# Crossbar transposes for a linear-attention hand-over, and new constants for a planned four-layer kernel

## The chip, the cores and the metric

The kernel runs on one core of a Trainium2 chip. The metric is the device time of one execution in microseconds (us). The core has five engines that run their own instruction lists: TensorE (PE, matrix products), VectorE (DVE), ScalarE (ACT), GpSimd (POOL) and SyncE (SP, which here only issues transfers). Sixteen DMA engines move data beside them. Matrix products land in PSUM, eight banks of 128 x 512 floats; everything else lies in SBUF.

## The reference, cut to what matters

Four layers run over one sequence of 2048 rows of 512 numbers: softmax attention (A), linear attention (B), A again, B again, each with a layer norm before it and a residual addition behind it. A has 32 query heads of 16 numbers and one shared key and value head.

```python
def _A_ref(x, wq, wk, wv, wo):            # H = 32, Dh = 16
    ...
    scores = jnp.einsum("bhqd,bkd->bhqk", q, k) * (Dh ** -0.5)
    p = _softmax(scores, axis=-1)
    o = jnp.einsum("bhqk,bkd->bhqd", p, v)
    ...
def _B_ref(x, wqkv, wo):
    ...
    kv = jnp.einsum("bhsd,bhse->bhde", pk, v)
    num = jnp.einsum("bhqd,bhde->bhqe", pq, kv)
    den = jnp.einsum("bhqd,bhd->bhq", pq, z)[..., None] + 1e-6
    ...
x = A_x
x = x + _A_ref(_layernorm(x, axis=-1), A_wq, A_wk, A_wv, A_wo)
x = x + _B_ref(_layernorm(x, axis=-1), B_wqkv, B_wo)
x = x + _A_ref(_layernorm(x, axis=-1), A_wq, A_wk, A_wv, A_wo)
x = x + _B_ref(_layernorm(x, axis=-1), B_wqkv, B_wo)
```

The dominant work is the exponential of 32 x 2048 x 2048 scores in each of the two softmax layers.

## The kernel before, in words

**Tiles.** The sequence is 16 tiles of 128 rows. In a softmax layer the scores are made in blocks of 128 keys x 512 columns, where a column is a query row of one of four heads. A layer has 32 segments (16 query tiles, times two halves of the heads) with 16 x 4 blocks each, which is 2048 blocks for a layer and 4096 for the kernel.

**Two ways for a block.** A score block (L990, four 32-row products beside each other on PE) leaves PSUM either through ACT or through DVE. ACT exponentiates two or three blocks with one instruction (L1170) into a tile named PT; one product (L1044) then multiplies it with the values. DVE takes a single block (L1256): it adds a constant and clamps, and the bits of the 16-bit integer, read as bf16, are a straight-line approximation of the exponential. Three more copies of it with an offset, each for four blocks at once (L1304), and a weighted sum of four products make the approximation good. One of these three copies can be made by DMA instead of DVE: POOL fills a buffer with the offset from a constant row in DRAM (L1328, "priming") and later issues a transfer that adds the block to it (L1337, an "addition"). Tile names in the trace are those of the memory that a buffer borrows: FB, xn, wq, wo, sacc, OBB and xnT all serve as such buffers for a while.

**The planner.** The order of each engine's instructions isn't written by hand. When the kernel is built, a class Planner (L36 to L353) plays the program through with a cost for each operation, a priority, and pools of banks and buffers; whenever a planned engine comes free, it takes the eligible operation with the lowest priority number. What comes out is one fixed list for each engine, with semaphore waits. So constants that look like costs change no instruction's speed; they change the order, which engine takes a copy, and how many blocks and copies go which way. Those that the change touches:

- SWITCH: what a change between PE's row, column and full tile shapes costs in the plan. STICK: how far the plan goes out of order to stay in one shape.
- TRS, TRT, DXF, DTAIL: how long a transposing DMA and an addition take in the plan. While a transposing DMA is in flight there, POOL starts no transfer (L158), and later POOL transfers wait for the last six of them (L200).
- BLS, BLT, BLO, DXB: how much work may be queued for DVE when it is given another block. A block gets there in three ways: as third member of a group whose banks belong to ACT, which leaves ACT two (dve_split, L1246, bounds BLS and BLT); as an additional member in a free bank (dve_open, L1240, BLO); or in a product of its own in a free bank (alone, L1266, DXB).
- FBO, FBS, FBP, AHEAD, NPRE, DQ, DMIN: how many buffers must be free for a new group of four, for a copy, for priming; how far ahead copies run; when an addition may be chosen (L1291: something is primed, the segment isn't among the last DMIN, and the planned DMA queue ends within DQ).
- CHE, CHT, ENDL, BACK: where DVE stops taking blocks ahead of a layer's end, and when borrowed weight buffers are called back. LAG: how close a more urgent operation must be for an engine to wait for it.

Constants set for layer 0 stay in force until layer 2 sets its own.

**The hand-over that the change is about.** It runs from layer 1 (linear) to layer 2 (softmax). Layer 1's sums over the keys need all 16 tiles of layer 0, so its second part, main(t), starts only when layer 0 is over. For a tile, main(t) multiplies the query side with the sums (L1838), divides into a tile OBB (L1842), transposes it in four 128 x 128 pieces on PE with an identity matrix (L1857), copies the result from PSUM to SBUF (L1860, recorded as L746; ACT or DVE, as the planner chooses), multiplies with the output weights (L761) and adds to x (L1870). Layer 2 follows for the same tile: statistics (L842, L843), two small POOL steps (L844, L846), the normalized tile xn (L849), four transposes on PE (L869), a copy into xnT (L874, recorded as L746), then the products for values, keys and queries (L757, L761, L923). Tiles 0 and 1 take a split path of their own (L789, L1824). From the third tile on, main(t) waits in the plan until layer 2's xnT of tile t-2 is there (MGATE, MLAG, L1796). In layer 2 ACT begins exponentials as soon as the first two key tiles are there, in the order of SEQ (L416): key tiles 0 and 1 for query tiles 0 and 1, then key tiles 2 and 3, then query tiles 2 and 3 on key tiles 0 to 3, then key tiles 4 to 7 for four query tiles, then 8 to 15. Keys are made for tiles 0, 1, 2-3, 4-7, 8-11 and 12-15 (KG, L417). DVE takes blocks only once the keys of tile 15 are there (KGATE).

**Transposes by DMA** are there already: dmat (L767) issues one from SP, and ln_tile(far) uses it for layer 0's tiles 4 to 15 (FARA, first entry). The same branches exist for layer 2 (FARA, second entry, L884) and for main(t) (FARM, L1848).

Of the kernel before, what the change touches and what calls it, by code (L numbers as in the profile page):

```python
# [35 lines left out]
class Planner:  # L36
# [43 lines left out]
    def op(self, opts, reads=(), writes=(), prio=5.0, lat=0.08, dma=False, name="", join=None, mode="full", port=False, after=(), behind=(), xfer=None, trn=False):  # L80

        o = Op()
        o.opts, o.prio, o.users, o.done, o.end = opts, prio, [], False, None
        o.eng, o.fn, o.n, o.value, o.sem, o.signal, o.isdma = None, None, None, None, None, False, dma
        o.name = (name, lat)
        o.freed = False
        o.begun = None
        o.cols = 0
        o.mode = mode
        o.port = port  # L90
        o.xfer = xfer
        o.trn = trn
        deps = set()
        for k in reads:
            deps.update(self.ws(k))
        for k in list(writes) + list(after) + list(behind):
            deps.update(self.ws(k))
            deps.update(self.readers.get(k, ()))
        if join is not None:
            deps.update(join.deps)  # L100
            deps.discard(join)
        for k in writes:
            if join is not None and join in self.ws(k):
                self.writer[k] = self.ws(k) + [o]
            else:
                self.writer[k] = [o]
                self.readers[k] = []
        for k in list(reads) + list(after):
            if k not in writes:
                self.readers.setdefault(k, []).append(o)  # L110
        o.deps = deps
        o.left = 0
        chain = len(opts) == 1 and PE in opts
        for d in deps:
            if not (d.done or (chain and d.freed and d.eng == PE)):
                o.left += 1
                d.users.append(o)
        if o.left == 0:
            self._eligible(o)
        return o  # L120
# [26 lines left out]
    def _dispatch1(self, e):  # L147
# [4 lines left out]
        while h:  # L152
# [24 lines left out]
            if e == PE:  # L177
                if self.mode != o.mode:
                    dur += max(SWITCH - (self.now - self.until[e]), ROWIN if o.mode == "row" else 0.0)
                self.mode = o.mode  # L180
# [13 lines left out]
            if o.trn:  # L194
                self.turning.append(o)
                self.turned = self.turned[-5:] + [o]
                self.dmaq = max(end, self.dmaq) + TRS
                end = self.dmaq + TRT
            if o.xfer:
# [156 lines left out]
class Seg:  # L356
# [11 lines left out]
    def take(self, js, back=False):  # L368
# [12 lines left out]
QK_DUR = 0.22  # L381
PV_DUR = 0.222
QK_LAT = 0.438
SWITCH = 0.107
ROWIN = 0.025
PV_LAT = 0.215
EX_LAT = 0.185
# [3 lines left out]
LAG = 0.15  # L391
# [7 lines left out]
DMAX = 1.0  # L399
RING = 24  # L400
NOB = 4
TRS = 1.4
TRT = 1.0
FARA = (4, 16)
FARB = 0
FARO = 0
FARM = {1: (), 3: ()}
GROW = (5,)
BLS = 1.4
BLO = 5.0  # L410
DXB = 2.0
BLT = 2.5
# [12 lines left out]
ENDL = 12  # L425
# [7 lines left out]
FBO = 2  # L433
FBS = 4
AHEAD = 20
CHT = 19
PSH = False
STICK = 0.8
PBL = 1.2
BACK = 2  # L440
PRING = 8
DSH = 1
DMIN = 4
NPRE = 2
EVEN = True
CHE = 8
AVOID = True
PGEN = 0.95
DPF = 1.7
DXF = 3.2  # L450
DTAIL = 2.0
DQ = 4.0
FBP = 4
TUNE = {0: {"CHE": 2, "AHEAD": 10, "BLS": 1.7, "FBP": 2, "NPRE": 1, "DMIN": 3, "LAG": 0.1, "STICK": 2.0, "FBO": 1, "FBS": 4, "BLO": 7.0, "DXB": 0.8, "BLT": 3.2},
        2: {"CHE": 6, "CHT": 16, "FBS": 2, "AHEAD": 15, "BLO": 3.5, "DXB": 2.5, "FBP": 3, "DMIN": 2, "STICK": 0.8, "LAG": 0.1, "DQ": 5.0}}


def bass_interleave_layers__grouped_kv_mqa__linear_attn_block__prompt_kernel(
# [111 lines left out]
    def guest(L, kind, i, h=None):  # L570
        return once((L, kind, i, h), home[kind, i]) if (kind, i) in home else ()
# [103 lines left out]
    def reload(dst, src, writes, prio, behind):  # L675
        return op({PO: (1.1, lambda e: e.dma_start(dst, src))}, writes=writes, prio=prio, lat=0.3, dma=True, behind=behind, xfer=(2.4, DTAIL))

# [34 lines left out]
    def fb_keys(i):  # L712
        return [("FB", i, h) for h in range(CHB)]
# [53 lines left out]
    def dmat(dst, src, reads, writes, prio, after=()):  # L767
        return op({SP: (0.1, lambda e: e.dma_start(dst, src, transpose=True))}, reads=reads, writes=writes, prio=prio, lat=0.5, dma=True, behind=after, trn=True)

    def until(*keys):  # L770
        for k in keys:
            yield ("ops", pl.ws(k))
# [105 lines left out]
    def a_tile(L, t, prio):  # L878
# [4 lines left out]
        cr = t in MCRIT[L - 1] if L else False  # L883
        yield from ln_tile(L, t, prio, t >= FARA[L // 2], cr)  # L884
        pl.flag(("xnT", L, t))
# [95 lines left out]
    def run_a(L):  # L981
# [23 lines left out]
        def spend(h, o):  # L1005
            h[0] -= 1
            if o not in h[1]:
                h[1].append(o)
            if h[0] == 0:
                pl.give_after(h[2], h[3], h[1])  # L1010
# [85 lines left out]
        def act_stream():  # L1096
            if L == 0:
                globals().update(TUNE[0])
            yield ("flag", ("K", L, 0))
            globals().update(TUNE[L])  # L1100
            if L:
# [214 lines left out]
        def prime():  # L1316
# [6 lines left out]
            while state["si"] < len(segs) - DMIN:  # L1323
                if len(primed) >= NPRE or len(fb_pool.free) <= FBP or fb_pool.wait:
# [3 lines left out]
                o = op({PO: (PGEN, lambda e, g_=g_: e.dma_start(fbs[g_].bitcast(I16), cst.to_broadcast([P, CHB * 512])))}, reads=["cst"], writes=fb_keys(g_), prio=9.0,  # L1328
                       lat=0.3, dma=True, behind=guest(L, "FB", g_), xfer=(DPF, DTAIL))
                primed.append((g_, o))  # L1330
# [4 lines left out]
        def dma_shift(blk, f_, hold, g_, o):  # L1335
            pl.stat["dma"] += 1
            o = op({PO: (PGEN, lambda e: e.dma_start(fbs[g_].bitcast(I16), fbs[f_].bitcast(I16), accum_op=ALU.add))}, reads=fb_keys(f_), writes=fb_keys(g_), prio=0.0, lat=0.3,  # L1337
                   dma=True, xfer=(DXF, DTAIL))
            spend(hold, o)
# [152 lines left out]
    def run_b(L):  # L1492
# [299 lines left out]
        def main(t):  # L1792
# [52 lines left out]
            pl.give_after(banks, b, [o])  # L1845
            if t not in FARM[L]:
                yield from until(("OB", i, 0), ("OB", i, 1))
            if t in FARM[L]:  # L1848
                dmat(OTB[:, i, :, :], OB[:, i, :], [("OB", i, 0), ("OB", i, 1)], [("OTB", i)], pr)
# [91 lines left out]
```

## Time and profile before

| | |
|---|---|
| median of 3 runs | 1484.73 us (1484.37 to 1490.2) |
| the profiled execution | 1484.35 us, its span 1482.5 us |
| PE, DVE, ACT busy | 1415.0, 1412.3 and 1441.2 us (95%, 95%, 97%) |
| POOL busy | 424.9 us (29%) |
| DMA moved | 240.14 MB |
| TensorE clock granted | 1.00 |

How to read it: an instruction's duration includes its own latency, and the next one on the engine can start before it ends, so the spacing of starts is the price of an instruction on a full engine, and it is less than the duration. Busy time counts overlapping durations once. PEld is the loading of weights, which goes beside the products of PE. A window row gives for each engine the busy time and the count in a stretch of the span. In a chain or timeline row the first number is the start, the second the length of a merged run of instructions, and a bracket tells of the idle time ahead of it and of what ended that.

### The profile page before, as it was taken

The page shows a single profiled execution, that of the slowest core. Times are in us where ns is not written, and L with a number is a line of the kernel's source. Part 1 is how long each engine was busy: PE and PEld are TensorE (multiplying, and loading weights), DVE is VectorE, ACT ScalarE, POOL GpSimd, SP SyncE. Part 2 cuts the span into 40 slices and gives each one's busy share as a digit, 9 for nine tenths or more (in the row PEclk, how much of TensorE's full clock was granted, in tenths as well). Part 3 has the DMA queues.
Part 4 walks back from the last instruction along what each step waited for, and adds up shares of the span by engine and source line. Part 5 has one row for each costly group of instructions (what it writes and reads, how often), then busy time and mean ns, then how long its engine had stood idle before and what let it go on. Part 6 is the DMA issues. An engine that isn't in the chain of part 4 may idle for free.

```text
span 1482.5 us, 40513 instructions
## 1 busy us (share of the span) xinstructions
PE 1415.0 (95%) x16387; PEld 512.6 (35%) x16387; DVE 1412.3 (95%) x2628; ACT 1441.2 (97%) x1536; POOL 424.9 (29%) x627
## 2 busy tenths in 40 slices
PE   7999999999999999999999999999999999999998
PEld 4433333333332323233644323333333333333235
DVE  7999999999999999998866899999999999999996
ACT  8999999999999999999799999999999999999996
POOL 5323333333333332300111223333323333223201
PEclk9999999999999999999999999999999999999999
DMA  4887898897888987710000458898879899879701
GB/s 116 229 205 194 185 212 188 203 215 179 195 204 197 217 192 168 187 43 2 2 2 2 104 136 200 201 211 205 212 188 226 201 211 215 203 183 216 172 1 58
DMA packets 76745, 240.14 MB, mean 162 GB/s; under 512 B 14993, under 2 KB 20113, under 8 KB 76562
## 3 DMA queue, kind: packets, MB, share of 16 engines
q0 software_dynamic: 62928, 229.14, 65.9%
q1 hardware_dynamic: 13634, 8.43, 2.0%
q8 instruction: 131, 2.15, 0.6%
q14 instruction: 52, 0.43, 0.1%
HBM read 120.62 MB, written 2.10 MB: 83 GB/s over the span
## 4 chain that ended last, share of the span: by engine, by line
PE 38%; DVE 35%; ACT 19%; issue 7%; POOL 1%; DMA 0%; ACTq 0%; DVEq 0%; POOLq 0%
PE ps L1044 15%; DVE FB L1256 14%; ACT PT L1170 12%; PE ps L990 12%; DVE FB L1304 7%; ACT xnT L1170 3%; PE ps L761 3%; PE ps L923 2%; PE ps L1089 2%; ACT OBB L1170 2%; PE ps L1410 2%; DVE wq L1256 1%; DVE xn L1256 1%; DVE sacc L1390 1%; PE ps L757 1%
## 5 line engine op out<-in xcount | busy, mean ns | idle before, releaser
L1170 ACT ACTIVATE PT<-ps 128x1024 bf16<-128x1024 f32 (+1 forms) x957 | 1004.8, 1163 | 5.4 <-PE ps L990 4.5
L1256 DVE TENSOR_SCALAR FB<-ps 128x512 int16<-128x512 f32 x852 | 558.0, 677 | 2.4 <-PE ps L990 1.6
L990 PE MATMUL ps<-QT,KM 32*128 32x512 bf16 x4096 | 534.6, 384 | 26.7 <-ACT PT L1170 14.9
L1044 PE MATMUL ps<-FB,VW 128*32 128x512 bf16 x3279 | 471.5, 385 | 10.9 <-ACT PT L1170 4.2
L1044 PE MATMUL ps<-PT,V 128*32 128x512 bf16 x2081 | 375.2, 386 | 4.0 <-DVE FB L1304 1.3
L990 PEld LDWEIGHTS ps<-QT,KM 32*128 32x128 bf16 x4096 | 134.2, 90 | 445.7 <-ACT PT L1170 216.0
L1170 ACT ACTIVATE xnT<-ps 128x1024 bf16<-128x1024 f32 (+1 forms) x240 | 261.0, 1162 | 1.0 <-PE ps L990 0.5
L1304 DVE TENSOR_SCALAR FB<-FB 128x2048 int16<-128x2048 int16 (+1 forms) x346 | 230.7, 674 | 0.0
L1337 POOL DMA_DIRECT2D FB<-FB x110 | 105.0, 955 | 334.3 <-DVE FB L1256 176.5
L1170 ACT ACTIVATE OBB<-ps 128x1024 bf16<-128x1024 f32 (+1 forms) x167 | 186.3, 1151 | 0.7 <-PE ps L990 0.6
L1044 PEld LDWEIGHTS ps<-FB,VW 128*32 128x32 bf16 x3279 | 115.8, 94 | 147.7 <-issue 81.3
L1328 POOL DMA_DIRECT2D FB<-shift_row x150 | 124.6, 831 | 45.2 <-PE ps L1044 23.9
L1089 PE MATMUL ps<-QT,V 128*32 128x512 bf16 (+6 forms) x548 | 132.7, 311 | 1.7 <-DVE sacc L1393 0.9
L1044 PEld LDWEIGHTS ps<-PT,V 128*32 128x32 bf16 x2081 | 91.3, 93 | 65.4 <-issue 36.7
L1044 PE MATMUL ps<-xnT,V 128*32 128x512 bf16 x522 | 105.1, 386 | 0.3 <-ACT PT L1170 0.3
L844 POOL TENSOR_SCALAR ve<-mv 128x1 f32<-128x1 f32 x64 | 29.5, 463 | 234.2 <-DVE mv L843 232.6
L1044 PE MATMUL ps<-OBB,V 128*32 128x512 bf16 x362 | 82.5, 387 | 1.8 <-ACT PT L1170 0.8
L761 PE MATMUL ps<-wqkv,xnT 128*32 128x512 bf16 x960 | 83.2, 383 | 0.8 <-DVE xnT L746 0.7
L1089 PEld LDWEIGHTS ps<-QT,V 128*32 128x32 bf16 x548 | 44.1, 95 | 56.8 <-issue 35.1
L1256 DVE TENSOR_SCALAR xn<-ps 128x512 int16<-128x512 f32 x80 | 52.7, 677 | 0.0
L1044 PE MATMUL ps<-xn,VW 128*32 128x512 bf16 x267 | 49.7, 385 | 1.8 <-ACT PT L1170 1.3
L1256 DVE TENSOR_SCALAR wq<-ps 128x512 int16<-128x512 f32 x75 | 49.3, 676 | 0.1
(221 smaller groups left out, 1805.8 us busy)
## 6 DMA issues: line engine op xcount, KB each, us to landing
FB<-shift_row POOLq DMA_DIRECT2D x150, 512.0 KB, 6.7
FB<-FB POOLq DMA_DIRECT2D x110, 512.0 KB, 6.0
sacc<-shift_row POOLq DMA_DIRECT2D x17, 512.0 KB, 6.9
wq<-shift_row POOLq DMA_DIRECT2D x16, 512.0 KB, 7.1
wo<-shift_row POOLq DMA_DIRECT2D x14, 512.0 KB, 7.1
xn<-shift_row POOLq DMA_DIRECT2D x14, 512.0 KB, 7.1
FB<-wq POOLq DMA_DIRECT2D x13, 512.0 KB, 6.1
wq<-FB POOLq DMA_DIRECT2D x12, 512.0 KB, 6.1
```

What stands on the lines that cost most here:

```text
L761: ins = e.matmul(dst[c, :], lhsT=l[:, c], rhs=r, start=(k == 0), stop=(k == len(pairs) - 1))
L844: op({PO: (0.1, lambda e: e.tensor_scalar(out=ve[:, t:t + 1], in0=mv[:, t, 1:2], scalar1=1e-5, scalar2=None, op0=ALU.add))}, reads=[("mv", ...
L923: ins = e.matmul(dst[:, g * P:(g + 1) * P], lhsT=lhs(g, k), rhs=rhs(k), start=(k == 0), stop=(k == FT - 1))
L990: return e.matmul(bank(b), lhsT=KM[r, sg.par, kt * P:(kt + 1) * P], rhs=QT[r, sg.t, :], start=True, stop=True)
L1044: ins = e.matmul(ps[32 * j:32 * j + 32, ACC * 512:(ACC + 1) * 512], lhsT=V[:, kt, :] if w is None else VW[:, kt, w, :], rhs=ap, start=(k = ...
L1089: o = op({PE: (n / 2400.0, lambda e: e.matmul(ps[32 * j:32 * j + 32, b * 512:b * 512 + n], lhsT=V0[:], rhs=QT[:, sg.t, 0:n], start=st, sto ...
L1170: ex = op({AC: (0.051 + 0.4267 * n, lambda e, n=n, s_=s_, p_=p_: e.activation(pts[p_][:, 0:n * 512], ps[:, s_ * 512:(s_ + n) * 512], ACTF. ...
L1256: o = op({DV: (0.602, lambda e: e.tensor_scalar(out=dst.bitcast(I16), in0=bank(b), scalar1=VB, scalar2=VLO, op0=ALU.add, op1=ALU.max))}, w ...
L1304: o = op({en: (du, lambda e, w=w, g_=g_: e.tensor_scalar(out=fbs[g_][:, 0:n].bitcast(I16), in0=fbs[f_][:, 0:n].bitcast(I16), scalar1=float ...
L1328: o = op({PO: (PGEN, lambda e, g_=g_: e.dma_start(fbs[g_].bitcast(I16), cst.to_broadcast([P, CHB * 512])))}, reads=["cst"], writes=fb_keys ...
L1337: o = op({PO: (PGEN, lambda e: e.dma_start(fbs[g_].bitcast(I16), fbs[f_].bitcast(I16), accum_op=ALU.add))}, reads=fb_keys(f_), writes=fb_k ...
L1410: o = op({PE: (0.12, lambda e, c=c: e.transpose(ps[:, b * 512 + c * P:b * 512 + (c + 1) * P], src[:, c * P:(c + 1) * P], identF[:]))}, rea ...
```

## The change

Only constants change; no instruction sequence is written differently. FARA's second entry goes from 16 to 2, so layer 2's tiles 2 to 15 are transposed by DMA (14 tiles). FARM of layer 1 names tiles 6 to 15, so main(t) transposes those by DMA (10 tiles). Together 24 of the 32 tile transposes of the hand-over leave PE, with the copies out of PSUM that follow them. The planned costs of a shape change, a transposing DMA and an addition are changed. The two sets of planning constants for the softmax layers are new; by the description of the change, the additions by DMA come to 194.

```diff
-SWITCH = 0.107
+SWITCH = 0.112
...
-TRS = 1.4
-TRT = 1.0
-FARA = (4, 16)
+TRS = 1.2
+TRT = 0.8
+FARA = (4, 2)
 FARB = 0
 FARO = 0
-FARM = {1: (), 3: ()}
+FARM = {1: (6, 7, 8, 9, 10, 11, 12, 13, 14, 15), 3: ()}
...
-DXF = 3.2
-DTAIL = 2.0
+DXF = 3.0
+DTAIL = 1.8
 DQ = 4.0
 FBP = 4
-TUNE = {0: {"CHE": 2, "AHEAD": 10, "BLS": 1.7, "FBP": 2, "NPRE": 1, "DMIN": 3, "LAG": 0.1, "STICK": 2.0, "FBO": 1, "FBS": 4, "BLO": 7.0, "DXB": 0.8, "BLT": 3.2},
-        2: {"CHE": 6, "CHT": 16, "FBS": 2, "AHEAD": 15, "BLO": 3.5, "DXB": 2.5, "FBP": 3, "DMIN": 2, "STICK": 0.8, "LAG": 0.1, "DQ": 5.0}}
+TUNE = {0: {"CHE": 4, "FBO": 1, "FBS": 2, "AHEAD": 10, "BLS": 1.0, "DXB": 1.6, "BLT": 3.2, "NPRE": 1, "STICK": 1.5, "BACK": 3, "ENDL": 6, "FBP": 5, "DMIN": 3, "DQ": 4.0, "LAG": 0.1},
+        2: {"CHE": 4, "FBO": 0, "BLO": 3.5, "FBP": 6, "DMIN": 4, "ENDL": 12, "FBS": 7, "DXB": 1.2, "DQ": 3.0}}
```

The lines that the constants steer, as they stand in both kernels:

```python
if t in FARM[L]:                                                              # L1848
    dmat(OTB[:, i, :, :], OB[:, i, :], [("OB", i, 0), ("OB", i, 1)], [("OTB", i)], pr)
...
yield from ln_tile(L, t, prio, t >= FARA[L // 2], cr)                         # L884
...
if far:                                                                       # L852
    o = dmat(xnT[:, :, cols], xn[:, i, :], [("xn", i)], [("xnT", c)], prio, hk)
```

## The prediction

> **What bounds the kernel now.** I read the page first, then busy times by stretch, then single operations.
>
> ```profile
> span 1482.5 us, 40513 instructions
> PE 1415.0 (95%) x16387; PEld 512.6 (35%) x16387; DVE 1412.3 (95%) x2628; ACT 1441.2 (97%) x1536; POOL 424.9 (29%) x627
> ...
> DVE  7999999999999999998866899999999999999996
> ACT  8999999999999999999799999999999999999996
> ```
>
> Three engines are near full, and the slices show one dent, at 18 to 22 of 40. The windows, cut there, give span length, then busy time and count of PE, PEld, DVE, ACT and POOL, then clock, DMA share and GB/s:
>
> ```profile
> 0.00:705.00 705.00, 668.71 (x7740) 230.90 (x7741) 689.09 (x1267) 692.89 (x727) 214.33 (x326) 1.00 0.74 175
> 705.00:830.00 125.00, 120.98 (x1484) 63.06 (x1481) 88.62 (x209) 113.10 (x125) 20.99 (x52) 1.00 0.02 6
> 830.00:1420.00 590.00, 568.63 (x6598) 190.22 (x6594) 587.88 (x1068) 586.81 (x617) 184.62 (x243) 1.00 0.82 193
> ...
> 745.00:830.00 85.00, 82.28 (x981) 36.63 (x978) 57.03 (x123) 84.53 (x78) 14.86 (x37) 1.00 0.02 8
> ```
>
> In the two long softmax stretches ACT and DVE are both over 97% busy, so neither bounds alone: they share the score blocks, and the time there is the sum of their work, dealt out evenly. The hand-over, 705 to 830, is different: DVE lacks 36 us, the DMA engines lie idle (0.02), PE and ACT are full. So work saved there is worth something on ACT, little on DVE.
>
> The exchange rate between the engines comes from three lines over the same three stretches: DVE's blocks (L1256), its copies with an offset (L1304), and POOL's additions (L1337); then ACT's groups (L1170) with their sum:
>
> ```profile
> 0.00:705.00 705.00, 387.13 (x592) 1.00 0.74 175
> 705.00:830.00 125.00, 0.69 (x1) 1.00 0.02 6
> 830.00:1482.50 652.50, 350.75 (x538) 1.00 0.75 178
> ```
> ```profile
> 0.00:705.00 705.00, 224.44 (x335) 1.00 0.74 175
> ...
> 830.00:1482.50 652.50, 199.20 (x304) 1.00 0.75 178
> ```
> ```profile
> 0.00:705.00 705.00, 104.29 (x109) 1.00 0.74 175
> ...
> 830.00:1482.50 652.50, 102.39 (x107) 1.00 0.75 178
> ```
> ```profile
> 0.00:705.00 705.00, 674.73 (x673) 1.00 0.74 175
> 705.00:830.00 125.00, 99.15 (x88) 1.00 0.02 6
> 830.00:1482.50 652.50, 600.39 (x605) 1.00 0.75 178
> sum 1482.50, ACT 1374.28; mean ACT 458.09
> ```
>
> DVE takes 1131 of the 4096 blocks and makes 639 copies; 216 copies are additions by DMA; ACT has 2965 blocks in 1366 groups, 1374.28 / 2965 = 0.46 us a block. The spacing on a full DVE stands in the chain, two instructions to a row, and on ACT in its timeline, where the second row starts 1.33 us after the three-block instruction that the first one begins with, and the third 0.91 us after the two-block one:
>
> ```profile
> 1058.77 1.20 DVE FB L1304 x2
> 1059.98 1.20 DVE FB L1256 x2
> ```
> ```profile
> 1106.92 2.38 ACT L1170 ACTIVATE PT<-ps 128x1536 bf16<-128x1536 f32 x2
> 1108.25 1.04 ACT L1170 ACTIVATE PT<-ps 128x1024 bf16<-128x1024 f32 x1
> 1109.16 0.63 ACT L1498 ACTIVATE phE<-ps 128x512 bf16<-128x512 f32 x1
> ```
>
> A block and a copy cost DVE 0.60 us each, so a DVE block with its copies costs 0.60 + 0.60 x 639/1131 = 0.94 us. ACT makes 1/0.46 = 2.17 blocks a us, DVE 1/0.94 = 1.06. One us of work more on a full DVE costs 1.06/3.23 = 0.33 us of time, one on ACT 0.67, as blocks move to the other engine.
>
> **The change part by part. Additions: +4.4 us.** I take the 194 as a count of the same thing as the 216. Then 22 copies return to DVE: 22 x 0.60 = 13.2 us, x 0.33 = 4.4. They are ordinary copies in the full stretches, so nothing hides them; 22 primings fewer save POOL and DMA time only, and POOL is 29% busy. If they fell into DVE's idle time: 0. Ends 0 and +4.4; I take 4.4.
>
> **Transposes: about 0.** First, what leaves PE. Here are a transpose of each kind with the product behind it:
>
> ```profile
> 760.38 0.40 PE L869 MATMUL ps<-ident,xn 128*128 128x128 bf16 x4
> 760.71 0.61 PE L761 MATMUL ps<-wo,OBB 128*32 128x512 bf16 x8
> ...
> 816.10 0.40 PE L1857 MATMUL ps<-ident,OBB 128*128 128x128 bf16 x4
> ...
> 816.34 0.39 PE L1838 MATMUL ps<-kvz,QT 128*128 128x128 bf16 x4
> ```
>
> Start to start that is 0.33 us with changes of tile shape and 0.24 without; 24 of them hold PE 5.8 to 7.9 us. Second, what the DMA adds: the twelve transposes of layer 0, from issue to landing, and the path of a tile as it is now.
>
> ```profile
> xnT<-xn SPq DMA_TRANSPOSE x12, 2.5
> ...
> DMA to landing us min/median/max: 2.4/2.5/4.0
> ```
> ```profile
> 750.00 0.40 PE L1838 MATMUL ps<-kvz,QT 128*128 128x128 bf16 x4
> 750.91 0.67 DVE L1842 TENSOR_TENSOR OBB<-ps,rdB 128x512 bf16<-128x512 f32 x1
> 752.45 0.62 ACT L746 COPY OBB<-ps 128x512 bf16<-128x512 bf16 x1
> 758.58 0.41 DVE L849 TENSOR_SCALAR xn<-x_sb,mv,rs 128x512 bf16<-128x512 bf16 x1 [0.42 <-POOL rs L846]
> 760.82 0.42 DVE L746 COPY xnT<-ps 128x512 bf16<-128x512 bf16 x1 [0.29 <-PE ps L869]
> 763.05 0.40 PE L1838 MATMUL ps<-kvz,QT 128*128 128x128 bf16 x4
> ```
>
> From OBB written (751.58) to its transpose copied (753.07) takes 1.5 us now, from xn (758.99) to xnT (761.24) 2.25 us, much of that waiting for a turn. By DMA both are about 2.7 us: 2.5 and 0.2 for a semaphore. That is +1.2 and +0.45 on the path of a tile. The last row is the main product of the second tile on, which the plan puts behind xnT (lag of two): 13.05 us for two tiles, 11.2 of them this path. If the path alone sets the pace, 10 tiles have both (+0.8 us each, half of 1.65) and 4 only the second (+0.2): +9 us until the keys are complete. If PE alone sets it: -8 us. PE at 82.28 of 85 us is as near to a bound as the path at 11.2 of 13.05, so I take +2.
>
> What a us of this stage is worth is small: ACT goes on with exponentials, and DVE only begins its blocks a us later, so 0.33 us: +0.7, ends -2.6 and +3.0. The copies that leave DVE there (0.41 us each) were hidden by its own idle time and are worth nothing. The few on ACT count. The copies of L746 in the three stretches, DVE then ACT:
>
> ```profile
> 705.00:830.00 125.00, 20.65 (x51) 2.51 (x5) 1.00 0.02 6
> ```
>
> Five on ACT, small ones among them; I estimate three that go, 1.9 us x 0.67 = -1.3. Against that, keys 2 and 3 come by DMA at a point where ACT waits for them: estimate 1 us, +0.7. Sum +0.1, ends -3.9 and +3.7.
>
> The issue of 24 transposes costs SP alone, which has nothing else between its first 40 us and the stores. Where POOL's next transfers wait for the last transposes, POOL's small steps queue behind them; at the end of the stage only two primings are due.
>
> *By the skill's prices:* the Trainium skill, page "VectorE: DVE Perf Modes", sections "The three transpose paths" and "Rules for kernel authors", gives 390 ns for a 128 x 128 transpose on TensorE and 1309 ns by DMA, and advises TensorE where PSUM will do. Four in a row by DMA would be an estimated 5.2 us; the trace has 2.5 us for all four and disagrees, so the rule enters only as a rival below.
>
> **New planning constants: -4.6 us, the softest term.** They can only change what goes where. The clear direction is BLS, 1.7 to 1.0: at 0.60 us a block, 1.7 let DVE take ACT's third block with two waiting, 1.0 with one. So more ACT groups keep three blocks: 0.443 us a block in place of 0.455. Of the 1366 groups 233 have three (2965 - 2 x 1366), 1133 two. No row says how many change. Ends: none (0), and all 2266 blocks (27 us of ACT, -18). The trace with its 233 is nearest to the low end; I take a quarter, 566 x 0.012 x 0.67 = -4.6. The buffer constants (FBP up, FBS, FBO) and the layer ends I set at nothing: the full stretches hold no idle time to win, and the only loss I can price is the second rival's.
>
> **Sum:** +4.4 + 0.1 - 4.6 = -0.1 us on the profiled execution, whose 1484.35 us are the span and 1.85 us around it, 0.4 under the median of the runs. Forecast 1484.3 us: no change that can be told. A measurement of this kernel tells about 0.5%, 7.4 us, from none.
>
> **The rivals.**
>
> *1. Faster: the groups widen and PE sets the hand-over.* Half of the two-block groups become three (-9.1), the stage shortens by 8 us (-2.6, and -1.3 on ACT): with +4.4, 1475.7 us. For it: PE is 97% full in the hand-over. Against: ACT is full there anyway, and DVE must still get its blocks some other way.
>
> *2. Slower: PE becomes the bound in the softmax stretches.* Blocks that DVE no longer takes from a group come in a product of their own (L1273), one more step of PE. Beside the row at 760.38 the score product starts at 760.06, so a step costs 0.32 us.
>
> ```profile
> 760.06 0.39 PE L990 MATMUL ps<-QT,KM 32*128 32x512 bf16 x2
> ...
> sum 1482.50, PE 132.67 PEld 44.07; mean PE 44.22 PEld 14.69
> ```
>
> PE idles 36 + 21 us in the two long stretches, and 130 us of the 132.67 are filler products there (L1089) that it can drop: 188 us at most, or 590 lone blocks. That is the point from which it decides. At 650, PE is 19 us over; groups widened by as many save 650 x 2 x 0.012 x 0.67 = 10.5: 1484.35 + 19 + 4.4 - 10.5 = 1497 us. Against it: layer 2's DXB falls, which makes lone blocks rarer there.
>
> *3. Slower: the keys come too late for ACT.* DVE's copies of layer 2's keys, with first and last start:
>
> ```profile
> L912 DVE TENSOR_SCALAR KM<-ps,kmask x7: 340/750/752, 723.5 to 831.2; 128x512 bf16<-128x512 f32 x6, 128x128 bf16<-128x128 f32 x1
> ```
>
> If transposes land in 4.0 us, the longest time above, the path grows by 4.65 us a tile, the stage by 14 x 2.3 = 33 us. From the first key copy at 723.5, ACT's exponentials begin at about 727 (estimate); ACT then has 256 blocks to do before it needs key tiles 8 to 15, 256 x 0.46 = 118 us and some waiting at the start, until about 848; the last keys are there at 832 now. 16 us of the 33 cost 0.33 each and 17 a whole us: 1484 + 22 = 1506. Against it: the transfers would find the DMA engines idle. The skill's 5.2 us would lie beyond this; the trace's 2.5 speaks against it.
>
> *4. The additions are not fewer in effect* (the 194 counts something else, or the copies land in idle time): the first term goes, 1480 us.
>
> **How the numbers follow.** Forecast 0.52 (its own range 1477 to 1491, where the ends of the transposes and half of the last term lie), rival 1 0.20, rival 2 0.13, rival 3 0.05, rival 4 0.10. Faster by over 0.5%: rival 1 and 0.03 of the forecast, 0.23. Slower: rivals 2 and 3 and 0.03, 0.21. Within: 0.56. The range 1473 to 1498 leaves out rival 3, half of rival 2 and a third of rival 1, 0.18 together.
>
> **What would show it.** Additions: L1337 at 194, copies of L1304 up by about 22 if DVE's blocks stay at 1131. Transposes: 36 DMA transposes, landing near 2.5 us; L869 down by 56 products and L1857 by 40; the last keys between 823 and 840. Constants: ACT's groups fewer than 1366 for about the same blocks; fillers of L1089 fewer. The forecast is wrong if ACT or DVE show idle time in the full stretches, if PE idles less than 2% there with no fillers left, or if the hand-over moves by more than 15 us.

## The result, and the profile after

The kernel after takes 1493.61 us (median; 1489.67 to 1495.79), the kernel before 1485.47 us beside it: ratio 1.0048, 95% interval 1.0036 to 1.0059, so 5.3 to 8.8 us slower. The forecast was no change; its wide range, 1473 to 1498, holds this time, the forecast's own, 1477 to 1491, does not. The profiled execution took 1494.09 us, 9.7 more than that of before.

The head of the page of the kernel after, with two rows of its slices:

```profile
span 1492.4 us, 40270 instructions
PE 1422.5 (95%) x16324; PEld 514.6 (34%) x16328; DVE 1402.0 (94%) x2592; ACT 1448.6 (97%) x1532; POOL 394.9 (26%) x583
...
DVE  7999999999999999999765799999999999999996
ACT  8999999999999999999799999999999999999996
```

DVE has 10 us less to do and ACT 7 us more, in a span 10 us longer: work went from DVE to ACT; copies coming back would have made DVE busier. DVE's dent is deeper. Its windows (span length; busy time of PE, PEld, DVE, ACT, POOL with counts; clock, DMA share, GB/s), cut at the hand-over:

```profile
0.00:705.00 705.00, 669.91 (x7716) 231.24 (x7717) 688.03 (x1264) 692.89 (x720) 208.69 (x318) 1.00 0.72 169
705.00:840.00 135.00, 127.47 (x1486) 64.52 (x1484) 83.18 (x189) 119.78 (x131) 19.42 (x49) 0.97 0.14 25
840.00:1430.00 590.00, 568.93 (x6560) 190.78 (x6558) 583.46 (x1054) 587.62 (x611) 162.53 (x211) 1.00 0.70 162
```

The long stretches look as before: the first has the same ACT time to 0.01 us. The hand-over has changed. It is cut ten us later here and holds about the same number of products (1486, 1484 before), but PE idles 7.5 us of it where it idled 4, ACT 15 where it idled 12, and the granted clock is 0.97. Its end is the last key copy, here in the rows of that line, count, duration and first and last start:

```profile
L912 DVE TENSOR_SCALAR KM<-ps,kmask x7: 351/751/752, 727.4 to 842.5; 128x512 bf16<-128x512 f32 x6, 128x128 bf16<-128x128 f32 x1
```

842.5 in place of 831.2. Its start is ACT's last copy of layer 0, here after and then before:

```profile
L776 ACT COPY OT<-ps x1: 366/366/366, 706.9 to 706.9; 128x256 bf16<-128x256 bf16 x1
```
```profile
L776 ACT COPY OT<-ps x1: 372/372/372, 705.0 to 705.0; 128x256 bf16<-128x256 bf16 x1
```

Between the two points the stage took 135.6 us in place of 126.2: layer 0 lost 1.9 us, the stage 9.4, and what follows won 1.4 back. The experiments below show that only about half of the 9.4 go with the transposes.

The added transposes, and who waited for them, in the hand-over of the kernel after:

```profile
L768 SPq DMA_TRANSPOSE xnT<-xn x14: 1189/1194/2379, 738.7 to 837.0; - x14
L768 SPq DMA_TRANSPOSE OBB<-OBB x10: 1189/1191/2139, 758.8 to 829.8; - x10
...
who waited for it (us, times):
...
  PE ps L757: 2.7, 3
...
  PE ps L761: 1.9, 2
...
DMA to landing us min/median/max: 2.3/2.4/4.4
```

The median landing is 2.4 us, much as the 2.5 of layer 0's transposes had led to expect, but some take up to 4.4, and PE, not only the path of a tile, waits for them. The longest of these waits, in the timeline of PE (start, length, bracket: idle time ahead and what ended it), and the same place in windows of 2 us:

```profile
788.81 0.40 PE L1044 MATMUL ps<-PT,V 128*32 128x512 bf16 x4
790.85 0.83 PE L761 MATMUL ps<-wo,OBB 128*32 128x512 bf16 x12 [1.64 <-DMA OBB<-OBB]
...
793.84 0.61 PE L990 MATMUL ps<-QT,KM 32*128 32x512 bf16 x3
...
795.54 1.89 PE L923 MATMUL ps<-xnT,wq 128*128 128x128 bf16 x16
...
800.59 0.39 PE L990 MATMUL ps<-QT,KM 32*128 32x512 bf16 x3
```
```profile
789.00:791.00 2.00, 0.36 (x8) 0.12 (x8) 0.29 (x1) 1.63 (x2) 0.00 (x0) 1.00 0.37 70
791.00:793.00 2.00, 2.00 (x29) 0.74 (x21) 0.61 (x1) 0.95 (x1) 0.00 (x0) 1.00 0.00 0
793.00:795.00 2.00, 2.00 (x16) 0.56 (x13) 1.97 (x6) 1.92 (x3) 0.45 (x2) 0.51 0.00 0
...
799.00:801.00 2.00, 2.00 (x17) 0.68 (x19) 0.00 (x0) 1.38 (x2) 0.00 (x0) 0.79 0.00 0
```

Two transposes were in flight (issued at 786.39 and 787.88); the first landed 4.4 us after its issue. PE stood still for 1.64 us (the loading of its weights for 1.94), and 2 us after it had gone on, its clock fell to half for 7 us: a score product that took 0.39 us takes 0.61. In the profiled execution of before the clock is 1.00 in every window of 5 us.

A second transpose in flight does not by itself make a landing late. Here are the transposes issued at 795.17 and 796.45, again two in flight, and then one issued at 752.30 with none in flight:

```profile
L768 SPq DMA_TRANSPOSE OBB<-OBB x1: 1191/1191/1191, 795.2 to 795.2; - x1
L768 SPq DMA_TRANSPOSE xnT<-xn x1: 1216/1216/1216, 796.4 to 796.4; - x1
...
DMA to landing us min/median/max: 2.3/2.4/2.4
```
```profile
L768 SPq DMA_TRANSPOSE xnT<-xn x1: 1413/1413/1413, 752.3 to 752.3; - x1
...
DMA to landing us min/median/max: 4.3/4.3/4.3
```

The pair landed in time and the lone one late. What makes some of them late stays open.

### The profile page after: what moved, and what is told of

It is laid out like the page before. It is cut to its first block, busy times and chain, and to the rows that moved or that the text cites. A ratio compares the mean times of both kernels' runs of the same rounds, so it can differ in the third digit from the quotient of the medians.

```text
span 1492.4 us, 40270 instructions
## 1 busy us (share of the span) xinstructions
PE 1422.5 (95%) x16324; PEld 514.6 (34%) x16328; DVE 1402.0 (94%) x2592; ACT 1448.6 (97%) x1532; POOL 394.9 (26%) x583
## 5 line engine op out<-in xcount | busy, mean ns | idle before, releaser
L1170 ACT ACTIVATE PT<-ps 128x1024 bf16<-128x1024 f32 (+1 forms) x958 | 1015.4, 1156 | 8.8 <-PE ps L990 7.0
L1256 DVE TENSOR_SCALAR FB<-ps 128x512 int16<-128x512 f32 x767 | 509.3, 684 | 3.1 <-PE ps L990 1.9
L1044 PE MATMUL ps<-FB,VW 128*32 128x512 bf16 x3229 | 457.3, 385 | 11.7 <-ACT PT L1170 3.3
L1044 PE MATMUL ps<-PT,V 128*32 128x512 bf16 x2104 | 381.2, 387 | 6.5 <-ACT PT L1170 3.0
L1170 ACT ACTIVATE xnT<-ps 128x1024 bf16<-128x1024 f32 (+1 forms) x239 | 263.7, 1138 | 1.3 <-PE ps L990 1.0
L1304 DVE TENSOR_SCALAR FB<-FB 128x2048 int16<-128x2048 int16 x319 | 214.9, 683 | 0.4
L1170 ACT ACTIVATE OBB<-ps 128x1024 bf16<-128x1024 f32 (+1 forms) x167 | 186.8, 1150 | 1.0 <-PE ps L990 1.0
L1337 POOL DMA_DIRECT2D FB<-FB x94 | 89.2, 949 | 340.7 <-DVE FB L1256 195.1
L1089 PE MATMUL ps<-QT,V 128*32 128x512 bf16 (+6 forms) x645 | 149.7, 309 | 0.2
L1044 PE MATMUL ps<-xnT,V 128*32 128x512 bf16 x516 | 112.8, 387 | 2.7 <-ACT xnT L1170 1.3
L1089 PEld LDWEIGHTS ps<-QT,V 128*32 128x32 bf16 x645 | 51.7, 95 | 64.3 <-issue 41.6
L1256 DVE TENSOR_SCALAR xn<-ps 128x512 int16<-128x512 f32 x108 | 71.9, 684 | 1.2 <-PE ps L990 1.1
L1256 DVE TENSOR_SCALAR wq<-ps 128x512 int16<-128x512 f32 x76 | 50.7, 685 | 1.2 <-PE ps L990 0.7
```

Of the source, the lines that this page charges most:

```text
L1044: ins = e.matmul(ps[32 * j:32 * j + 32, ACC * 512:(ACC + 1) * 512], lhsT=V[:, kt, :] if w is None else VW[:, kt, w, :], rhs=ap, start=(k = ...
L1089: o = op({PE: (n / 2400.0, lambda e: e.matmul(ps[32 * j:32 * j + 32, b * 512:b * 512 + n], lhsT=V0[:], rhs=QT[:, sg.t, 0:n], start=st, sto ...
L1170: ex = op({AC: (0.051 + 0.4267 * n, lambda e, n=n, s_=s_, p_=p_: e.activation(pts[p_][:, 0:n * 512], ps[:, s_ * 512:(s_ + n) * 512], ACTF. ...
L1256: o = op({DV: (0.602, lambda e: e.tensor_scalar(out=dst.bitcast(I16), in0=bank(b), scalar1=VB, scalar2=VLO, op0=ALU.add, op1=ALU.max))}, w ...
L1304: o = op({en: (du, lambda e, w=w, g_=g_: e.tensor_scalar(out=fbs[g_][:, 0:n].bitcast(I16), in0=fbs[f_][:, 0:n].bitcast(I16), scalar1=float ...
```

## The experiments

Three theories stood against each other. **Theory 1:** the loss lies in the hand-over: waits on landings, a longer stage, the clock that falls. **Theory 2:** it lies in the planning constants and the fewer additions. **Theory 3:** any order dealt anew loses some us against the order of before, whatever the change is for. Each comparison was run beside the kernel before:

| kernel | median us | ratio to before, 95% interval | at clock 1.000 |
|---|---|---|---|
| before | 1485.2 | | 1484.6 |
| after | 1493.61 | 1.0036 to 1.0059 | 1490.6 |
| e1: after, no added transposes | 1490.24 | 1.0017 to 1.0039 | 1489.2 |
| e2: before, with the transposes | 1492.15 | 1.0029 to 1.0056 | 1491.7 |
| e3: after, nobody waits for a landing | 1490.71 | 1.0023 to 1.0051 | 1488.2 |
| e4: before, planned costs only | 1491.32 | 1.0024 to 1.0045 | 1488.2 |
| c1, c2, c3: before, orders dealt anew | 1489.26, 1489.08, 1488.89 | 1.0010 to 1.0037 | 1486.6, 1486.7, 1486.3 |
| c4: before, no additions | 1527.84 | 1.0272 to 1.0299 | 1524.0 |
| e5: after, the longest wait filled | 1494.07 | 1.0043 to 1.0092 | 1491.2 |
| e6: before, one wait in the hand-over | 1489.00 | 1.0012 to 1.0043 | 1487.0 |
| e7: before, one wait in softmax | 1492.74 | 1.0039 to 1.0066 | 1489.5 |
| s1, s2: before, constants searched | 1475.27, 1480.10 | 0.9917 to 0.9941, 0.9950 to 0.9975 | 1475.0, 1478.9 |
| s3, s4: after, constants searched | 1487.92, 1492.05 | 1.0001 to 1.0037, 1.0031 to 1.0057 | 1484.1, 1489.1 |

The last column is worked out: executions of one kernel differ in their mean clock, and their times go with it. The kernel before takes a median of 1484.6 us at clock 1.000, 1486.6 at 0.998 and 1488.0 at 0.997. One straight line through all runs of all kernels, with a level of its own for each kernel, has a slope of 1.04 us for each 0.001 of the clock, and the runs scatter about 1.1 us around it (one run of e1 at 0.949 is left out). The column is no better than some tenths of a us, and it allows for the mean clock alone.

**e1, the kernel after without the added transposes.**

```diff
-FARA = (4, 2)
-FARM = {1: (6, 7, 8, 9, 10, 11, 12, 13, 14, 15), 3: ()}
+FARA = (4, 16)
+FARM = {1: (), 3: ()}
```

> The changed kernel with the 24 transposes back on PE (FARA's second entry 16, FARM empty); all other new constants stay, the additions too. Theory 1 (the loss lies in the hand-over: PE waits for transposes to land, the stage grows, the clock falls in the gaps): the last keys come near 833 us in place of 843, no clock under 1.00, time 1485 to 1487. Theory 2 (the loss lies in the new constants and the fewer additions): 1491 to 1494, as with the transposes. Theory 3 (any other order than the one of before loses some us, since the constants of before were picked for their own order): 1487 to 1491.

1490.24 us, with 194 additions; the last keys (a copy by ACT) come at 837.1, and the stage takes 131.0 us. So about 4.2 us (2.5 to 5.8; 4.6 at equal clock) come with constants and additions alone, and about 3 more with the transposes, 1.4 of them at equal clock. Of the 9.4 us by which the stage grew, 4.8 are there without the added transposes. Theory 1 had said 1485 to 1487: the hand-over is not the whole of the loss.

**e2, the kernel before with the transposes** and their planned cost:

```diff
-TRS = 1.4
-TRT = 1.0
-FARA = (4, 16)
-FARM = {1: (), 3: ()}
+TRS = 1.2
+TRT = 0.8
+FARA = (4, 2)
+FARM = {1: (6, 7, 8, 9, 10, 11, 12, 13, 14, 15), 3: ()}
```

> The kernel before with the 24 transposes by DMA and their two planned costs (TRS 1.2, TRT 0.8) and nothing else; additions stay near 216. Theory 1: 1490 to 1495, the last keys near 840, a clock mean under 1.000. Theory 2: 1484 to 1487. Theory 3: 1487 to 1490.

1492.15 us, with 218 additions and the clock at 1.000 in the profiled execution: 6.2 us (4.3 to 8.3) for the transposes with the order that comes with them, more than in the kernel after. Theory 1 had the time right and the lower clock wrong. PE waited there 1.10 to 1.18 us at a time for landings.

**e3, the order of the kernel after, but PE waits for a transpose's source in place of its landing** and multiplies a resident tile:

```diff
 for d in o.deps:
+    deps.update(d.deps if e == PE and d.trn and d.name[0] == "free" else [d])
...
-pairs = [(OTB[:, i, g, :], wo2[:, g, :]) for g in range(4)]
+pairs = [(wqkv[:, g, 0:P] if t in FARM[L] else OTB[:, i, g, :], wo2[:, g, :]) for g in range(4)]
```

> The changed kernel in exactly its own order, all 36 transposes issued, but PE doesn't wait for the 24 of the hand-over to land: it waits for their source tile and multiplies a resident weight tile of the same shape in place of the transposed one, so the output isn't the reference's. Theory 1: the gaps in front of those products go, the last keys come 6 to 10 us earlier than 843, the clock stays at 1.000, time 1483 to 1487. Theory 2: 1490 to 1494, no change. Theory 3: in between, 1487 to 1490.

1490.71 us, the stage 129.9 us in place of 135.6. The waits on landings are worth 2.9 us of the kernel after by the medians, 2.4 at equal clock; this is the cleanest comparison, since no instruction changed its place. Theory 1 had said 1483 to 1487 at a clock of 1.000; the mean clock of the runs is 0.997, no higher than the 0.998 of the kernel after. So the lower clock of this order does not come from these waits alone.

**e4, the kernel before with the new planned costs alone:**

```diff
-SWITCH = 0.107
-DXF = 3.2
-DTAIL = 2.0
+SWITCH = 0.112
+DXF = 3.0
+DTAIL = 1.8
```

> The kernel before with only the planned costs of a shape change and of an addition as in the changed kernel (SWITCH 0.112, DXF 3.0, DTAIL 1.8); old sets of constants, transposes on PE. Theory 1: 1483 to 1487. Theory 2, in the part that blames the fewer additions: additions rise here (cheaper in the plan), so 1481 to 1485. Theory 3: 1488 to 1492, although nothing in it is an operation that costs more.

1491.32 us, though it has 228 additions, 12 more than before. In the profiled executions its hand-over is 3.2 us shorter than that of before (123.0 us); 4.0 us are lost in layer 0 and 7.2 behind the hand-over. So a new order can lose as much with no hand-over that grows. That asked for a control.

**c1, c2, c3, the kernel before with one planned cost moved by a hair,** which means nothing and only deals the order anew (212 to 215 additions). One line in each:

```diff
-SWITCH = 0.107
+SWITCH = 0.1065
...
-SWITCH = 0.107
+SWITCH = 0.1075
...
-EX_LAT = 0.185
+EX_LAT = 0.186
```

> A control: the kernel before with the planned cost of a shape change at 0.1065 in place of 0.107 (half a nanosecond, which is no change of substance in any direction). The order is dealt anew from there on. Theory 1 or 2 (the loss has a cause in the edits): as before, 1484 to 1487. Theory 3 (any order dealt anew is some us slower than the one of before, for which its constants were picked): 1487 to 1491.

> The second control: the planned cost of a shape change at 0.1075. Theory 1 or 2: 1484 to 1487. Theory 3: 1487 to 1491.

> The third control, through another constant: the planned latency of ACT's exponential (EX_LAT) 0.186 in place of 0.185. Theory 1 or 2: 1484 to 1487. Theory 3: 1487 to 1491.

All three lose 2.1 to 2.6 parts in a thousand, 3 to 4 us; about 2 us at equal clock, the rest by a lower clock. Their hand-overs take 129 to 132 us without any added transpose by DMA. And their clock falls with no wait of the length seen in the kernel after: in c1 PE idled 1.46 of the 3.41 us ahead of such a drop, with no idle time over 0.98 us.

```profile
258.91:262.32 3.41, 1.95 (x24) 0.58 (x25) 2.65 (x6) 3.41 (x4) 2.66 (x4) 1.00 1.02 272
262.32:265.73 3.41, 3.41 (x26) 1.30 (x26) 2.35 (x4) 1.80 (x2) 0.89 (x1) 0.50 0.85 216
```

Theory 3 holds for these orders, and some of what e1, e2 and e4 lose is no more than that.

**c4, the kernel before with no additions.** In layer 0's constants, which layer 2 keeps here:

```diff
-"NPRE": 1
+"NPRE": 0
```

> The kernel before without any addition by DMA (NPRE 0 for both softmax layers, so nothing is primed): all 216 copies go back to DVE, DMA is nearly idle. This measures the price of one addition on a scale far above the difference between orders. By the prediction's rate (0.60 us of DVE x 0.33) 216 additions are worth 43 us: 1528. If additions cost something that the rate leaves out (buffers, POOL, DVE held up), less: 1505 to 1520.

42.9 us for 216 additions are 0.199 us each, 39.4 and 0.18 at equal clock; the prediction's rate, 0.60 x 0.33 = 0.198, is right to a tenth.

**e5, the kernel after, its longest wait filled.** Seven products go ahead of the wait at 790.85:

```diff
+if fill is not None and d.trn and waited.get(k, 0) < d.value:
+    fill(eng)
...
+    o.warm = lambda e: [e.matmul(dst, lhsT=wqkv[:, 0, 0:P], rhs=wo2[:, 0, :], start=True, stop=True) for _ in range(warm)]
```

> The kernel after with its own order on every engine and all its waits. Only ahead of the longest wait of TensorE on a landing (tile 10 of layer 1, 1.94 us before 790.85 us in the profile after) TensorE now makes seven products of 512 columns, about 1.5 us of them, into the bank that the waiting product overwrites. The result is the reference's. Theory 1 (what costs is less the wait than the half clock that followed it, about 7 us at half speed, some 3.5 us of TensorE time): the drop at 793 to 800 us is gone, mean clock 1.000 in most runs, time about 1490.0, 3 to 4 us under the kernel after. Rival 1 (the wait itself and the order cost, the clock only happens to be low there): the wait's end is where it was, time 1493 to 1494. Rival 2 (the drop isn't set off by the wait): the clock still falls somewhere between 785 and 800, time 1493 to 1494.

The timeline of PE in e5 at that place:

```profile
789.16 1.68 PE L769 MATMUL ps<-wo,wqkv 128*128 128x512 bf16 x7
790.77 0.83 PE L764 MATMUL ps<-wo,OBB 128*32 128x512 bf16 x12
...
795.02 1.07 PE L928 MATMUL ps<-xnT,wq 128*128 128x128 bf16 x16
```

The wait is full and the clock stays: sixteen products take 1.07 us, not the 1.89 of the kernel after. But the time did not follow: 1494.07 us, with a lower clock in most runs, and in the profiled one it fell at 30 to 35 us, where e3 and e4 lose theirs too. That the kernel's time hangs on this one place was wrong. Nor is it shown that filling the wait kept the clock up: each kernel has one profile, and in four of the nine runs of the kernel after the mean clock is 0.999 or 1.000, too high for 7 us at half clock (0.0023 of the span), though the order is the same.

**e6 and e7, the kernel before with one wait more,** near 785 and near 400 us:

```diff
+d = pl.op({SP: (0.1, lambda e: e.dma_start(spare[:], wqkv[:, 0, 0:3 * P], transpose=True))}, dma=True, trn=True, prio=99.0)
+d.deps = {next(o for o in reversed(pe[:n]) if o.end <= pe[n].end - 0.7), *pl.ws("wqkv")}
+pe[n].deps.add(d)
```

> The kernel before with its own order. In the hand-over, near 785 us, one product waits in addition for a transposing DMA of three 128 x 128 blocks into a tile that nobody reads, which SP issues when a product some 0.7 us earlier is done: one wait of TensorE of about 2 us, as the kernel after has one there. Theory 1 (a TensorE wait of this length costs its full length where ACT is full, and sets off a drop of the clock): 2 us of wait and up to 3.5 us of lost clock, 1487 to 1490.5, clock 0.997 to 0.999 in most runs. The prediction's rate (0.33 us of time a us of this stage): +0.7 us, 1486.1. Rival (waits of this size are taken up by the buffers, what the kernel after lost is its order alone): no change, 1485.0 to 1485.6.

> The same as the last, but near 400 us, in the middle of the first softmax stretch, where ACT and DVE are full and TensorE idles 5 per cent. Theory 1: the wait costs up to its own 2 us, since ACT and DVE run out of score blocks, and a drop of the clock up to 3.5 us more, which is worth less here since TensorE has some idle time: 1486 to 1489. Rival (the clock falls only in the hand-over, with its changes of tile shape): clock 1.000 in most runs, 1485.5 to 1487.5. If the spare time of TensorE takes the wait up: 1485.0 to 1485.6.

PE in e6, and windows around it:

```profile
790.60 1.47 PE L762 MATMUL ps<-wo,OBB 128*32 128x512 bf16 x12 [1.89 <-DMA spare<-wqkv]
792.00 0.61 PE L991 MATMUL ps<-QT,KM 32*128 32x512 bf16 x3
```
```profile
787.00:789.00 2.00, 1.51 (x17) 0.32 (x14) 0.26 (x2) 2.00 (x3) 0.00 (x0) 1.00 0.00 0
789.00:791.00 2.00, 0.40 (x4) 0.14 (x8) 1.14 (x2) 0.98 (x2) 0.00 (x0) 0.74 0.24 49
791.00:793.00 2.00, 2.00 (x23) 0.46 (x19) 0.00 (x0) 0.00 (x0) 0.00 (x0) 0.50 0.00 0
```

One wait of 1.89 us makes the kernel 4 us slower (1.8 to 6.4): 2.4 us at equal clock, the rest by clock. Its profiled execution shows all of it in the order of before: a wait as in the kernel after, 10 us at half clock from within the wait on, and ACT without work for 3.66 us, as its timeline in e6 says:

```profile
793.64 2.37 ACT L1171 ACTIVATE PT<-ps 128x1536 bf16<-128x1536 f32 x2 [3.66 <-PE ps L1045]
```

In e7 the wait came out longer than meant:

```profile
408.21 0.61 PE L1045 MATMUL ps<-wq,VW 128*32 128x512 bf16 x2 [6.30 <-DMA spare<-wqkv]
```
```profile
402.00:404.00 2.00, 0.00 (x0) 0.00 (x0) 1.07 (x3) 0.23 (x1) 0.00 (x0) 1.00 1.12 186
404.00:406.00 2.00, 0.00 (x0) 0.00 (x0) 0.00 (x0) 0.00 (x0) 0.00 (x0) 0.95 0.91 168
406.00:408.00 2.00, 0.00 (x0) 0.00 (x0) 0.00 (x0) 0.00 (x0) 0.00 (x0) 0.50 0.58 186
```

The transpose was issued while additions filled the DMA engines (share 1.12) and landed after 6.5 us, against 2.4 in e6. PE, DVE and ACT all stood still; 7.9 us slower (5.8 to 9.8), 4.9 at equal clock, above everything that had been expected. PE's idle 5 per cent did not make it good.

**s1 to s4: the constants searched.** Still open was whether the transposes lose in any order, or only in one not picked. Some thousand sets of layer constants were tried in the planner for each side, the best two taken by where its list ends, the planned costs left as they were; the change is the content of TUNE alone. The edit of s1, cut to its core:

```diff
-TUNE = {0: {"CHE": 2, "BLS": 1.7, "FBP": 2, "DMIN": 3, "FBO": 1, "BLO": 7.0,
...
-        2: {"FBS": 2, "BLO": 3.5, "DXB": 2.5, "FBP": 3, "DMIN": 2, "STICK": 0.8,
...
+TUNE = {0: {'CHE': 4, 'BLS': 11.774, 'FBP': 0, 'DMIN': 1, 'FBO': 0, 'BLO': 11.171,
...
+        2: {'FBS': 0, 'BLO': 61.894, 'DXB': 2.0, 'FBP': 1, 'DMIN': 0, 'STICK': 1.152,
```

> The kernel before (no added transposes, its planned costs) with new planning constants for both softmax layers, picked among some thousand sets by where the planner's own list ends, none of them run on the chip. About 234 additions. Additions at 0.199 us each: 18 more save 3.6 us. Theory (the order of the kernel before was picked on the chip, any new order loses 2 to 4 us): 1483 to 1486. Rival (what the planner's list gains the chip gains too): 1476 to 1480.

> The same, from another start of the same search: about 237 additions, 21 more than before. Additions alone: -4.2 us. With a re-deal's loss of 2 to 4 us: 1482.5 to 1485. Rival (the chip follows the planner's list): 1479 to 1482.

> The kernel after, with its 24 transposes by DMA and its planned costs, and planning constants from a search of the same length. About 234 additions, 40 more than the kernel after: -8 us. If the transposes cost in any order: 1 us or more above s1 and s2, 1485 to 1488. If they cost only in an unpicked order: level with s1 and s2.

> The same from another start: about 219 additions, 25 more than the kernel after: -5 us, so 1487 to 1490 if nothing else changes. Above s1 and s2 by 3 us or more for 16 additions fewer; more than that is the transposes' own cost.

s1 beats both kernels, 10.5 us (8.8 to 12.3) under before, of which its 18 additions more explain 3.6. So theory 3 in its strong form, that the order of before can't be matched by a new one, falls: an order dealt blindly lost, a searched one won, and s1 and s2 came out beside the numbers of the rival. s1 and s3 have 234 additions each, and s3, with the transposes, is 12.7 us slower, 9.1 at equal clock. The keys, in s1 and then in s3:

```profile
L911 DVE TENSOR_SCALAR KM<-ps,kmask x7: 343/751/752, 721.2 to 826.6; 128x512 bf16<-128x512 f32 x6, 128x128 bf16<-128x128 f32 x1
```
```profile
L911 DVE TENSOR_SCALAR KM<-ps,kmask x6: 484/750/751, 738.3 to 838.9; 128x512 bf16<-128x512 f32 x5, 128x256 bf16<-128x256 f32 x1
```

Hand-overs of 123.2 and 136.6 us. And s3 has the wait, in its timeline of PE, with products at 0.61 us from 812.79 to 814:

```profile
809.76 0.40 PE L760 MATMUL ps<-wo,OBB 128*32 128x512 bf16 x4 [1.56 <-DMA OBB<-OBB]
...
812.79 0.61 PE L989 MATMUL ps<-QT,KM 32*128 32x512 bf16 x3
```

s4 has 219 additions and is 16.8 us over s1, of which 15 additions explain 3. The kernels with the transposes are slower in four comparisons, by 1.4 us at equal clock (after against e1, within what an order dealt anew moves) up to some 11 (s4 against s1, the additions allowed for). But s1 and s2, both without them, differ by 3.9 us at equal clock. How much is the transposes' own and how much the luck of an order is not settled; in none of these orders do they gain. So theory 1 holds in part, for the waits that e3 and e6 isolate; theory 2 holds for the additions and for constants that brought nothing; and theory 3 holds as a scatter of 3 to 4 us that every comparison here has to bear, except e3, e5, e6 and e7, which keep the order.

## Why the prediction was wrong

**Additions, +4.4: right.** The 194 are the count of L1337, and c4 gives their price (22 of them 4.0 to 4.4 us). But they did not come back as copies on DVE. The rows of the kernel after for DVE's blocks (L1256), copies (L1304) and ACT's groups (L1170):

```profile
0.00:700.00 700.00, 387.61 (x587) 1.00 0.72 170
700.00:840.00 140.00, 0.39 (x1) 0.98 0.14 24
840.00:1492.40 652.40, 347.01 (x524) 1.00 0.64 150
```
```profile
0.00:700.00 700.00, 224.25 (x332) 1.00 0.72 170
700.00:840.00 140.00, 2.40 (x7) 0.98 0.14 24
840.00:1492.40 652.40, 206.05 (x304) 1.00 0.64 150
```
```profile
0.00:700.00 700.00, 673.54 (x670) 1.00 0.72 170
700.00:840.00 140.00, 107.79 (x95) 0.98 0.14 24
840.00:1492.40 652.40, 600.78 (x601) 1.00 0.64 150
sum 1492.40, ACT 1382.11; mean ACT 460.70
```

643 copies, 4 more than before, and 1111 blocks, 20 fewer (one that crosses a cut stands in two rows): DVE gave blocks to ACT, which is the exchange that the rate stands for.

**New constants, -4.6: wrong, the first step that failed.** A quarter of the two-block groups was to widen; the groups are 1364 in both kernels (the rows above, and the 1366 of the prediction, count two twice, at the cuts). By their forms 258 are three wide in place of 237, which makes room for just the blocks that came over from DVE. So a lower BLS did not widen groups beyond that. No run changes BLS alone, but s1 has it at 11.8 in layer 0 and still 1366 groups and 1137 blocks on DVE; that the balance of the two engines sets this number is likely and not shown. e1, with all constants and the 194 additions, is 4.2 us slower, 4.6 at equal clock, which is the additions' 4.4 and nothing to set against it. The prediction also priced a new order at nothing beside that. c1 to c3 show that an order alone is worth 3 to 4 us, 2 at equal clock, and s1 that it can be worth several the other way; no term here is known better than that.

**Transposes, +0.1: wrong, the second step.** Between PE alone (-8) and the path alone (+9) I took +2 for the stage; it grew by 9.4, which looks like the path's end and is not: e1 has 4.8 of it without the added transposes, so 4.7 go with them, and e3 takes 5.7 away. PE had less to do but was not let go on: it waits for the landing of a tile, and some landings take over 4 us where the path was built on 2.5. At the prediction's rate 4.7 to 5.7 us of stage are 1.6 to 1.9 us of time; measured are 1.4 (after less e1) and 2.4 (after less e3) at equal clock. So the term that was to be +0.1 is 1.4 to 2.4. The rate is no law of the stage, though: e2's stage grew 5.2 us, worth 1.7 by it, and e2 lost 6.2; e4's shrank by 3.2, and e4 lost 5. The rate holds for work moved between ACT and DVE. A wait of PE can cost its full length: e6 lost 2.4 us at equal clock for 1.89 us of wait.

**The clock was missing.** The prediction read 1.00 in every window and took it as given. The kernel after stands 6.0 us over before at equal clock; some 2 of the 8.1 us between the medians are clock. It is no effect of the landings alone: e3 has the lower clock without those waits, c1 to c3 without added transposes, while e1 and e2 keep 0.999 in the mean.

**The sum as measured:** additions 4.4, constants with the new order 0.2, transposes 1.4, clock 2.1, together 8.1 in place of -0.1. The last two terms and the missing gain from the constants make the miss. That the sum closes follows from how it is split; how the 4.6 of e1 divide between additions and order is known to some 2 us.

**Rivals.** The third had the mechanism, landings that lengthen the stage, but needed 4.0 us for each; here few took that, and the stage grew by 9, not 33. (The 33 were too many even so: only 10 of the 14 tiles have both transposes by DMA, which makes about 27.) The second did not come: fillers rose from 132.67 to 149.65 us of PE time instead of vanishing. The first found no wider groups.

**What was to show it:** L1337 at 194, 56 and 40 products fewer in L869 and L1857 and the 2.4 us in the median came as said. Fewer groups, fewer fillers and 22 more copies did not. The last keys at 842.5 lay past the 823 to 840, the stage's 9.4 within the 15 us that were to prove the forecast wrong: that bound was too wide for a kernel where 7 us can be told.

## What to carry to other kernels

Moving work from a full engine to an idle queue puts a landing into the path; before counting what the engine saves, ask whether the engine itself waits for the landing, what the latest landing costs and not the median one, and what runs dry behind it. In a kernel whose order a planner deals, run controls that change nothing before believing an effect of some tenths of a per cent; here they moved the time by 3 to 4 us. And when a change adds planning constants, the constants may be worth more than the change: s1 gained 10 us with none of the transposes.

## What the runs showed of the hardware

- **Idle time of PE well under 3 us can go with a fall of its clock.** With an idle time of 1.89 us (e6) and after one of 1.64 us (after) the granted clock was 0.50 for 10 and 7 us; in s3 after 1.56 us for 3.4. It takes no single long wait: c1 lost its clock with no idle time over 0.98 us, after 3.41 us in which PE idled 1.46. And it does not follow each time: s4 kept 1.00 after PE had idled 1.4 of 3.4 us at 275 us, e2 after idle times of 1.1 to 1.2 us, and e3, e4 and e5 lost theirs at 30 us after 3.4 us in which PE was 83% busy. What sets it off stays open. The Trainium skill, page "TensorE: Matmul & The Clock Gate", section "Why this matters for your kernels", asks for no idle gaps of PE beyond about 3 us; e6 and c1 disagree, where the longest ahead of the fall were 1.89 and 0.98 us. The same page, in "A second HAM failure mode: psum-queue depth-cycling", speaks of short idles that make the clock swing, which agrees better with c1.
- **The falls come in steps.** In the profiled executions each lasts 3.41, 6.83 or 10.24 us (the end of the span apart), in softmax stretches as in hand-overs.
- **A transposing DMA lands in 2.3 to 2.5 us on nearly idle DMA engines, with or without another in flight; some take up to 4.4 us** (after). One issued while additions filled the DMA engines took 6.5 us (e7, a single one).
- One profiled execution of e1 shows a clock of 0.95 throughout and yet took 1491.7 us, where the other eight runs took 1489.0 to 1491.1.
